# Attention pairs handled in groups of two, and weight sums formed in place, in a fused attention and feed-forward kernel

## The chip, the cores and the metric

The kernel runs on one core of one Trainium2 chip. The metric is the device time of one execution in microseconds. The kernel before took 860.98 us in the median of three runs (858.56 to 863.52).

## The reference

Sparse attention over 8 batches, 8 heads, 576 positions and head size 64, then a feed-forward layer on the result. Half of the heads look at the last 32 positions ("local"), half at earlier positions that are equal modulo 32 ("strided"):

```python
scores = scale * np.matmul(q, k.transpose(0, 1, 3, 2))
mask_local = (rel >= 0) & (rel < 32)
mask_strided = (rel >= 0) & (pos[None, :] % 32 == pos[:, None] % 32)
attn = softmax(np.where(masks, scores, -1e9))          # max subtracted, 1e-9 added to the sum
x = (attn @ v).transpose(0, 2, 1, 3).reshape(4608, 512)
h = x @ w_in                                           # 512 -> 2048
out = (h * sigmoid(1.702 * h)) @ w_out                 # 2048 -> 512
```

All arrays are float32.

## The kernel before, in words

The feed-forward matmuls use a Strassen-Winograd scheme with seven products in place of eight. Each float32 operand is split into a high and a low fp32r part, and a product is three matmuls per half of the contraction (high x high, high x low, low x high), six in all. The core's TensorE (PE) does one such group of six matmuls, 288 columns wide, per *step* `s` of a long list. Everything else is hung onto the steps: `side(s, f, ...)` puts `f` behind the product of step `s`, and every engine keeps the order in which the calls are made (`InOrder`). So the numbers given to `side` set the order on VectorE (DVE), ScalarE (ACT), GpSimd (POOL) and on SyncE's DMA queue (SP).

The stages:

- Start: the attention of batch 0, with filler matmuls.
- Steps 0 to `HEAD` - 1 = 60, and three more after it: batch 0 times `w_in` without Strassen (`plain`, 64 units of six matmuls each sum in two pieces), while the `w_in` words are turned into fp32 and split: `w_scale`, `w_low`, `w_join`, `w_high`, `w_low_part`. Each weight `i` is also stored to DRAM (`plains`) and read back later (`t_load`) into an area of the tile `sums`, where POOL forms four differences (`t_sums`), which ACT and DVE split into the weights `wv[i][:, 3:7]` (`t_high`, `t_low`).
- From step `HEAD`, seven passes of 56 steps, one for each batch 1 to 7: `product(n, k)`, k = 0 to 6, for n = 8 b + i. Product n starts at step 5 + 7 n and has a product at every second step, so two n are interleaved and each step has one product. The banks are `mx`, `my`, `mz` of set n % 2; `combine` empties them (ACT for k = 0 and 2, DVE for the others) and stores to `hid` in DRAM. A product that accumulates onto a bank has to wait until `combine` has read it: k = 5 in `my`, four steps after k = 3, is one.
- During the pass of batch b the attention of batch b + 1 is worked in six *pairs* (two 96-query chunks, or two sets of residues, of four heads), three local ("l") and three strided ("s"). The steps of a pair: `scores` (PE, into the PSUM banks `s0`, `s1`), `masked` and `maxima` (DVE), `below` (POOL subtracts the maximum), `exps` (ACT), `totals` (DVE), `scaled` (POOL), `turn` (PE transposes into `s0`, ACT copies out to `pts`), `values` (PE into `s0`, `s1`, ACT copies out into the blocks of the next x). `scores` and `values` are many small matmuls on parts of the PE array: 64 rows x 32 columns for local scores, 64 x 64 (or 54 x 64) for the rest.
- At the end of a pass the seven sums x of the next batch are made: `x_sum` (1, 2 on DVE; 3, 4 on POOL), `x_high` (ACT), `x_low` (DVE).
- Last: 72 groups of 42 matmuls with `w_out`, 256 columns wide; here a scheduler sets the order.

Of the kernel before, what the change touches and what calls it, by code (L numbers as in the profile page):

```python
# [9 lines left out]
F32 = mybir.dt.float32  # L10
# [46 lines left out]
def _pairs():  # L57
    out = []
    for b in range(B):
        x = [[(kind, b, U * i) for i in range(PAIRS // 2)] for kind in "ls"]  # L60
        out += x[0] + x[1] if b == 0 else [u for i in range(PAIRS // 2) for u in (x[1][i], x[0][i])]
    return out
# [8 lines left out]
def attn_ffn(ctx, tc, qk, vs, weights, masks, ident, out):  # L71
# [102 lines left out]
    def pr_of(p):  # L174
        return prs[(1, 2, 3, 0, 4, 5)[p] if p < PAIRS else p % 2]
# [39 lines left out]
    def scores(p, banks):  # L215
# [27 lines left out]
    def parts_of(p, banks):  # L243
# [6 lines left out]
            bank[:nq, : 4 * WL].rearrange("p (i n) -> p i n", i=4)[:, :, :nk] for bank in banks  # L250
# [14 lines left out]
    def masked(p, banks):  # L265
        nq, nk, mask, pr, heads, srcs, (nmax, _, _) = parts_of(p, banks)
# [54 lines left out]
    def values(p, banks, shared=False):  # L321

# [5 lines left out]
        for g in range(2):  # L328
            for w, (q0, n, _, nk) in enumerate(windows(kind)):
                if kind == "s":  # L330
                    n = min(n0, (w + 1) * WS) - w * WS
                for u in range(U):
                    i = U * g + u
                    o = g * n0 + (q0 if kind == "l" else w * WS)
                    for j in range(2):
# [6 lines left out]
                        )  # L342
        x = {k: xr[k].rearrange("p (g n) -> p g n", g=2) for k in ("11", "12", "21", "22")}
        for u in range(U):
            src = banks[u][:, : 2 * n0].rearrange("p (g n) -> p g n", g=2)
            copy = vector.tensor_copy if shared and u else scalar.copy
            if kind == "l":
                h, o = divmod(c + u, 3)
                copy(out=x[("11", "21")[h]][:, :, o * QL : (o + 1) * QL], in_=src)
                continue  # L350
            n, r0, half = RES[c], R0[c + u], NPOS // 2
            src = src.rearrange("p g (r t) -> p g t r", r=n)
            for k, h in enumerate(("12", "22")):
                o = x[h].rearrange("p g (t r) -> p g t r", r=STRIDE)[:, :, :, r0 : r0 + n]
                copy(out=o, in_=src[:, :, k * half : (k + 1) * half])
# [32 lines left out]
    KINDS = (0, 4, 1, 5, 3, 6, 2)  # L388
# [43 lines left out]
    def t_sums(i):  # L432
        b11, b21, b22, b12 = (t_view(0)[:, q] for q in range(4))
        t1, t2, t3, t4 = (t_view(1 + i % 2)[:, q] for q in range(4))
        for o, x, y in ((t1, b12, b11), (t2, b22, t1), (t3, b22, b12), (t4, b21, t2)):
            gpsimd.tensor_tensor(out=o, in0=x, in1=y, op=ALU.subtract)

    def t_high(i):
        scalar.copy(out=wv[i][:, 3:7, 0], in_=t_view(1 + i % 2))

    def t_low(i):
        hi, lo = (wv[i][:, 3:7, s] for s in range(2))
        vector.tensor_tensor(out=lo, in0=t_view(1 + i % 2), in1=hi.bitcast(F32), op=ALU.subtract)
# [3 lines left out]
    six = [m_banks[i][x] for x in ("mx", "my", "mz") for i in range(2)]  # L447
# [3 lines left out]
    def plain(n, u):  # L451
# [3 lines left out]
        bank = six[1 + 2 * f if j >= 4 * FP - 2 else j % 6][:, :HALF]  # L455
# [93 lines left out]
    for i in range(n0 + 3):  # L549
# [7 lines left out]
        if i >= 3:  # L557
            values(i - 3, s_banks, i == n0 + 2)
# [43 lines left out]

    for b in range(B):
        at = first(b)
        if b == 1:
            for t, f, k in ((-8, x_sum, 1), (-7, x_sum, 3), (-6, x_high, 4), (-5, x_low, 4),
                            (-5, x_sum, 2), (-4, x_high, 1), (-3, x_low, 1), (-3, x_high, 0),
                            (-2, x_low, 0), (-1, x_high, 2), (0, x_low, 2), (1, x_sum, 4),
                            (2, x_high, 3), (3, x_low, 3), (4, x_high, 6), (5, x_low, 6),
                            (6, x_high, 5), (7, x_low, 5)):  # L610
                side(at + t, f, k, b)
        elif b:
            side(at - 11, x_sum, 1, b)
            side(at - 10, x_sum, 3, b)
# [6 lines left out]
        for i in range(PAIRS if b + 1 < B else 0):  # L621
            p = (b + 1) * PAIRS + i
            s = at + 4 + 6 * i if b > 1 else at - 3 * b + 7 * i + 2 * (not b)
            t = (4, 5, 6, 9, 11) if b > 1 else (4, 5, 6, 11, 12) if b and not i else (5, 6, 7, 10, 12)
            side(s, scores, p, s_banks)
            side(s, load_qk, p + 2)
            for f, d in ((masked, 0), (maxima, 1), (below, 2), (exps, t[0]), (totals, t[1]), (scaled, t[2])):
                side(s + d, f, p, s_banks)
            side(s + t[3], turn, p, s_banks[0])
            side(s + t[4], values, p, s_banks)  # L630
            side(s + t[4], load_v, p + 2)
# [4 lines left out]
    for i in range(2, FP):  # L636
        at = 7 * (i - 2) + 4
        if i > 2:
            side(max(0, 7 * (i - 3) - 3), load_w, i)
# [324 lines left out]
```

## Time and profile before

| | before |
|---|---|
| time of the profiled execution | 858.98 us |
| its span, first to last instruction | 857.0 us |
| median of the runs | 860.98 us (858.56 to 863.52) |
| mean granted clock of TensorE | 0.993 |
| PE busy | 838.0 us (98% of the span) |
| PE weight loads busy | 808.8 us (94%) |
| DVE, POOL, ACT busy | 549.7, 490.9, 426.9 us |

The span starts with the first instruction and ends with the last; the 1.98 us between it and the execution's time lie around it. Busy times of one engine don't overlap with themselves, those of different engines do. In lists of instructions in order of time the columns are the start and the length in microseconds, engine, line, operation, what is written and read, the shape, and how many instructions the row merges; in brackets stands the idle time before them and what ended it. All recorded operations have the line of the helper `ordered`, so the tiles' names tell them apart: `mx`, `my`, `mz`, `s` are PSUM banks, `xa` the split x, `w` the split weights, `arena` most of the working memory.

### The profile page before, as it was taken

The page shows a single profiled execution, that of the slowest core. Times are in us where ns is not written, and L with a number is a line of the kernel's source. Part 1 is how long each engine was busy: PE and PEld are TensorE (multiplying, and loading weights), DVE is VectorE, ACT ScalarE, POOL GpSimd, SP SyncE. Part 2 cuts the span into 40 slices and gives each one's busy share as a digit, 9 for nine tenths or more (in the row PEclk, how much of TensorE's full clock was granted, in tenths as well). Part 3 has the DMA queues.
Part 4 walks back from the last instruction along what each step waited for, and adds up shares of the span by engine and source line. Part 5 has one row for each costly group of instructions (what it writes and reads, how often), then busy time and mean ns, then how long its engine had stood idle before and what let it go on. Part 6 is the DMA issues. An engine that isn't in the chain of part 4 may idle for free. (4 is left out here: it accounts for less than half of the span.)

```text
span 857.0 us, 23992 instructions
## 1 busy us (share of the span) xinstructions
PE 838.0 (98%) x9827; PEld 808.8 (94%) x9827; DVE 549.7 (64%) x867; ACT 426.9 (50%) x666; POOL 490.9 (57%) x509
## 2 busy tenths in 40 slices
PE   7899999999999999999999999999999999999997
PEld 4799898999999999999999999999999999999997
DVE  5575776965857658558577775665565565566662
ACT  4675444433444434434446564655555655655540
POOL 2233866242332342423344358999998998777760
PEclk9999999999999999999999999999999999999999
DMA  8897576576685765766768853444433433443430
GB/s 330 289 395 282 174 234 222 164 254 210 205 265 175 242 212 189 253 215 203 223 233 259 266 195 109 152 159 127 146 123 124 146 126 124 141 131 123 136 106 31
DMA packets 112239, 164.84 MB, mean 192 GB/s; under 512 B 9729, under 2 KB 88321, under 8 KB 111105
## 3 DMA queue, kind: packets, MB, share of 16 engines
q1 hardware_dynamic: 112128, 163.31, 58.5%
q8 instruction: 77, 1.26, 0.6%
q14 instruction: 34, 0.27, 0.1%
HBM read 104.55 MB, written 58.72 MB: 191 GB/s over the span
## 5 line engine op out<-in xcount | busy, mean ns | idle before, releaser
L87 POOL TENSOR_TENSOR arena<-arena 128x256 f32<-128x256 f32 (+1 forms) x302 | 332.3, 1117 | 127.3 <-ACT arena L87 54.5
L87 DVE TENSOR_TENSOR xa<-arena,xa 128x576 fp32r<-128x576 f32 (+2 forms) x100 | 158.8, 1589 | 87.6 <-ACT xa L87 56.4
L87 PE MATMUL my<-xa,w 128*128 128x288 f32 x1140 | 180.3, 300 | 0.5 <-DVE arena L87 0.4
L87 ACT ACTIVATE arena<-arena 128x1024 f32<-128x1024 f32 (+2 forms) x120 | 105.4, 878 | 125.7 <-DMA arena<-hid 93.7
L87 PEld LDWEIGHTS my<-xa,w 128*128 128x128 f32 x1140 | 158.7, 189 | 3.3 <-DVE arena L87 1.0
L87 ACT CAST xa<-arena 128x576 fp32r<-128x576 f32 (+2 forms) x102 | 115.5, 1147 | 38.2 <-PE s L87 25.1
L87 PE MATMUL mx<-xa,w 128*128 128x288 f32 x804 | 132.0, 301 | 2.5 <-DVE w L87 1.0
L87 PE MATMUL mz<-xa,w 128*128 128x288 f32 x792 | 128.4, 300 | 0.0
L87 ACT COPY arena<-mx 128x288 f32<-128x288 f32 (+1 forms) x136 | 53.7, 395 | 143.0 <-PE mx L87 107.9
L87 PEld LDWEIGHTS mx<-xa,w 128*128 128x128 f32 x804 | 113.5, 190 | 4.9 <-DVE w L87 1.3
L87 DVE TENSOR_TENSOR arena<-my,arena 128x288 f32<-128x288 f32 (+1 forms) x204 | 90.0, 446 | 41.0 <-PE my L87 39.3
L87 PEld LDWEIGHTS mz<-xa,w 128*128 128x128 f32 x792 | 110.9, 188 | 1.5
L87 POOL TENSOR_TENSOR arena<-arena,rinv 96x512 f32<-96x512 f32 (+1 forms) x48 | 49.5, 1031 | 107.6 <-DVE rinv L87 64.3
L87 DVE TENSOR_TENSOR arena<-mz,arena 128x288 f32<-128x288 f32 (+1 forms) x166 | 71.7, 441 | 51.8 <-PE mz L87 50.0
L87 ACT COPY arena<-s 128x90 f32<-128x90 f32 (+4 forms) x184 | 51.3, 340 | 82.5 <-PE s L87 82.1
L87 DVE TENSOR_TENSOR ga<-arena,ga 128x1792 fp32r<-128x1792 f32 (+1 forms) x25 | 57.4, 2297 | 51.6 <-ACT ga L87 40.6
L87 POOL TENSOR_TENSOR arena<-arena,nmax 128x432 f32<-128x432 f32 (+1 forms) x42 | 46.3, 1103 | 76.7 <-DVE nmax L87 72.7
L87 PE MATMUL mz<-w_out,xa 128*128 128x256 f32 x576 | 75.5, 280 | 0.0
L87 PE MATMUL mx<-w_out,xa 128*128 128x256 f32 x576 | 75.4, 280 | 0.0
L87 PE MATMUL my<-w_out,xa 128*128 128x256 f32 x576 | 75.3, 280 | 0.0
L87 PEld LDWEIGHTS mx<-w_out,xa 128*128 128x128 f32 x576 | 71.1, 188 | 0.0
L87 PEld LDWEIGHTS my<-w_out,xa 128*128 128x128 f32 x576 | 71.0, 188 | 0.0
(72 smaller groups left out, 1000.8 us busy)
## 6 DMA issues: line engine op xcount, KB each, us to landing
hid<-arena SPq DMA_DIRECT2D x256, 144.0 KB, 3.2
arena<-hid SPq DMA_DIRECT2D x144, 256.0 KB, 3.3
arena<-qk SPq DMA_DIRECT2D x23, 448.0 KB, 4.5
arena<-qk SPq DMA_DIRECT2D x21, 472.0 KB, 4.4
arena<-vs SPq DMA_DIRECT2D x23, 384.0 KB, 4.6
out<-arena SPq DMA_DIRECT2D x34, 256.0 KB, 2.9
raw<-w_in SPq DMA_DIRECT2D x8, 1024.0 KB, 10.1
stage<-w_out SPq DMA_DIRECT2D x16, 512.0 KB, 5.1
```

The lines of the kernel that those rows point to most:

```text
L87: ins = call(*args, **kw)
```

## The change

1. **Pairs in groups of two.** The local and the strided pair of a group are scored in one step, side by side in the banks `s0`, `s1` (columns 0 and 256). The values of both pairs stand in one step, ahead of the scores of the next group, and go to two product banks, `mx1` and `mz0`, instead of `s0`, `s1`. So a step that held one of `scores` or `values` of one pair now holds up to four of them. Each pair's `turn` has a step of its own, as before, three and one (two for batch 1) steps ahead of the values. `moved` holds the copies out of the values. The local pair comes first.
2. **`plain` uses four banks in place of six** (the other two hold values), and DVE copies out for weights 0 to 4, ACT for 5 to 7 (before: one half each).
3. **Weight sums in place.** Each `plains[i]` is read into one of three areas, and the four differences overwrite it. The steps of load, four sums, high and low part come from a table, counted from `HEAD` (`T_STEPS`; one `t_sum(i, m)` is one difference), and the order of the weights is another (`KINDS`). For n = 8, product 1 goes ahead of product 0.
4. **Weights are prepared every 6 steps** in place of 7, and `w_low_part` of weights 1 to 7 runs on POOL in two halves. For batch 1, `x_low` of 4 and 6 runs on POOL, and the steps of its sums are earlier.

```diff
-        return prs[(1, 2, 3, 0, 4, 5)[p] if p < PAIRS else p % 2]
+        return prs[(1, 2, 3, 0, 4, 5)[p] if p < PAIRS else 1 - p % 2]
...
-    def scores(p, banks):
+    def scores(p, banks, at=0):
-                        banks[j][q0 : q0 + n, i * WL : i * WL + nk],
+                        banks[j][q0 : q0 + n, at + i * WL : at + i * WL + nk],
...
-                            banks[u][j * D : (j + 1) * D, o : o + n],
+                            banks[u][j * D : (j + 1) * D, at + o : at + o + n],
+        return lambda u: moved(p, u, banks[u][:, at : at + 2 * n0], shared)
...
-    def w_low_part(i):
-        hi, lo = (wv[i][:, 0:4, s] for s in range(2))
-        vector.tensor_tensor(out=lo, in0=words[i], in1=hi.bitcast(F32), op=ALU.subtract)
+    def w_low_part(i, some=slice(0, 4)):
+        hi, lo = (wv[i][:, some, s] for s in range(2))
+        (gpsimd if i else vector).tensor_tensor(
+            out=lo, in0=words[i][:, some], in1=hi.bitcast(F32), op=ALU.subtract
+        )
...
-        sync.dma_start(out=t_view(0), in_=plains[i].rearrange("p (q n) -> p q n", q=4))
+        sync.dma_start(out=t_view(i % 3), in_=plains[i].rearrange("p (q n) -> p q n", q=4))
-        for o, x, y in ((t1, b12, b11), (t2, b22, t1), (t3, b22, b12), (t4, b21, t2)):
+        o, x, y = ((b11, b12, b11), (b12, b22, b12), (b22, b22, b11), (b21, b21, b22))[m]
+        gpsimd.tensor_tensor(out=o, in0=x, in1=y, op=ALU.subtract)
...
-    six = [m_banks[i][x] for x in ("mx", "my", "mz") for i in range(2)]
+    four = [m_banks[0]["mx"], m_banks[0]["my"], m_banks[1]["my"], m_banks[1]["mz"]]
+    v_banks = [m_banks[1]["mx"], m_banks[0]["mz"]]
-            (vector.tensor_copy if f else scalar.copy)(out=h, in_=bank)
+            (vector.tensor_copy if n < 5 else scalar.copy)(out=h, in_=bank)
...
+    def both_scores(q):
+        for i in range(2):
+            scores(q + i, s_banks, 256 * i)
+            load_qk(q + i + 2)
+    def both_values(p):
+        moves = []
+        for i in range(2):
+            moves.append(values(p + i, v_banks, False, 216 * i))
+            load_v(p + i + 2)
+        for u in range(U):
+            for move in moves:
+                move(u)
+    def groups_of(b, slots):
+        for g in range(3):
+            q, s, then = b * PAIRS + 2 * g, slots[g], slots[g + 1]
+            side(s, both_scores, q)
+            for i in range(2):
+                side(s + i, masked, q + i, s_banks, 256 * i)
+                for f, d in (
+                    (maxima, 0), (below, 0), (exps, 4), (totals, 5 + i), (scaled, 5 + i)
+                ):
+                    side(s + d + i, f, q + i, s_banks)
+                side(then - (3, 2 if b == 1 else 1)[i], turn, q + i, s_banks[i])
+            side(then, both_values, q)
...
+            groups_of(b + 1, [at + t for t in ((3, 16, 30, 44) if b else (3, 17, 32, 47))])
...
-        at = 7 * (i - 2) + 4
+        at = 6 * (i - 2) + 4
+        for t in (0, 2):
+            side(at + 6 + t, w_low_part, i, slice(t, t + 2))
+    T_STEPS = (
+        (-19, (-15, -14, -13, -12), -10, -5), (-18, (-10, -9, -8, -7), -4, 1),
```

Three places in the order of the instructions show what moved.

PE, in a pass, around the values of a first group (`s0`, `s1`: scores, and before also values; `ident`: `turn`; rows with `xa` and `w`: a product of six matmuls). Before:

```order
L87 MATMUL s0_82<-arena_66 64x32 x2
...
L87 MATMUL mz0_78<-xa_67,w_2_636 128x288 x6
L87 MATMUL s0_82<-arena_66 32x64
...
L87 MATMUL my1_80<-xa_67,w_3_757 128x288 x6
L87 MATMUL my0_77<-xa_67,w_2_636 128x288 x6
L87 MATMUL mx1_79<-xa_67,w_3_757 128x288 x6
L87 MATMUL s0_82<-ident_sb_72,arena_66 128x128 x4
L87 MATMUL mz0_78<-xa_67,w_2_636 128x288 x6
L87 MATMUL my1_80<-xa_67,w_3_757 128x288 x6
L87 MATMUL s0_82<-arena_66 64x54 x2
...
L87 MATMUL mx0_76<-xa_67,w_4_874 128x288 x6
L87 MATMUL s0_82<-arena_66 64x54
```

Now:

```order
L87 MATMUL s0_82<-ident_sb_72,arena_66 128x96 x4
L87 MATMUL mx0_76<-xa_67,w_2_670 128x288 x6
L87 MATMUL mz1_81<-xa_67,w_1_550 128x288 x6
L87 MATMUL s1_83<-ident_sb_72,arena_66 128x128 x4
L87 MATMUL my0_77<-xa_67,w_2_670 128x288 x6
L87 MATMUL mx1_79<-arena_66 64x32 x2
...
L87 MATMUL mx1_79<-arena_66 64x54 x2
...
L87 MATMUL s0_82<-arena_66 32x64
...
L87 MATMUL s0_82<-arena_66 64x54
...
L87 MATMUL my1_80<-xa_67,w_1_550 128x288 x6
```

Four runs of small matmuls, each between products, became one: local values (64x32), strided values (64x54 and the like), local scores (32x64), strided scores (64x54). A batch has 4 such runs (scores; values and scores; the same; values) where it had 12; the six `turn` stay apart.

DVE, at the first steps of a pass (`xa`: `x_low`; `s0`, `s1` and `nmax`: `masked` and `maxima`; `my`, `mz`: `combine`). Before:

```order
L87 TENSOR_TENSOR arena_66<-my1_80,arena_66 128x288
L87 TENSOR_TENSOR xa_67<-arena_66,xa_67 128x576
L87 SCALAR_TENSOR_TENSOR arena_66<-s0_82,masks_sb_71 128x4x54
L87 SCALAR_TENSOR_TENSOR arena_66<-s1_83,masks_sb_71 128x4x54
L87 TENSOR_TENSOR arena_66<-mz1_81,arena_66 128x288
L87 TENSOR_TENSOR xa_67<-arena_66,xa_67 128x576
L87 TENSOR_REDUCE nmax_30_3989<-arena_66 128x8
L87 TENSOR_TENSOR arena_66<-my0_77,arena_66 128x288
L87 TENSOR_TENSOR xa_67<-arena_66,xa_67 128x576
```

Now:

```order
L87 TENSOR_TENSOR arena_66<-my1_80,arena_66 128x288
L87 TENSOR_TENSOR xa_67<-arena_66,xa_67 128x576
L87 SCALAR_TENSOR_TENSOR arena_66<-s0_82,masks_sb_71 96x4x64
L87 SCALAR_TENSOR_TENSOR arena_66<-s1_83,masks_sb_71 96x4x64
L87 TENSOR_REDUCE nmax_30_4011<-arena_66 96x8
L87 SCALAR_TENSOR_TENSOR arena_66<-s0_82,masks_sb_71 128x4x54
L87 SCALAR_TENSOR_TENSOR arena_66<-s1_83,masks_sb_71 128x4x54
L87 TENSOR_REDUCE nmax_31_4027<-arena_66 128x8
L87 TENSOR_TENSOR arena_66<-mz1_81,arena_66 128x288
L87 TENSOR_TENSOR xa_67<-arena_66,xa_67 128x576
L87 TENSOR_TENSOR arena_66<-my0_77,arena_66 128x288
```

Two pairs are masked in a row, ahead of the same `combine` of `mz1` and `my0`; `x_low` and `combine` keep their steps.

POOL, around step `HEAD` (`sums`: `t_sum`; 128x576: `x_sum` 3 and 4, with `xa` `x_low`; `nmax`: `below`; `rinv`: `scaled`; `w_7`: `w_low_part`). Before:

```order
L87 TENSOR_TENSOR arena_66<-arena_66,rinv_11_1147 96x4x128
L87 TENSOR_TENSOR sums_1273<-sums_1273 128x256 x4
L87 TENSOR_TENSOR arena_66<-arena_66 128x576
L87 TENSOR_TENSOR sums_1273<-sums_1273 128x256 x4
L87 TENSOR_TENSOR arena_66<-arena_66,nmax_12_1403 128x4x2x54
L87 TENSOR_TENSOR arena_66<-arena_66 128x576
```

Now:

```order
L87 TENSOR_TENSOR w_7_1170<-raw_7_901,w_7_1170 128x2x256 x2
L87 TENSOR_TENSOR sums_1206<-sums_1206 128x256 x4
L87 TENSOR_TENSOR arena_66<-arena_66 128x576
L87 TENSOR_TENSOR sums_1206<-sums_1206 128x256 x4
L87 TENSOR_TENSOR xa_67<-arena_66,xa_67 128x576
L87 TENSOR_TENSOR sums_1206<-sums_1206 128x256 x5
L87 TENSOR_TENSOR arena_66<-arena_66 128x576
L87 TENSOR_TENSOR sums_1206<-sums_1206 128x256
L87 TENSOR_TENSOR arena_66<-arena_66,nmax_12_1497 96x4x128
```

Between the two `x_sum` of batch 1 (rows 128x576) stood four sums; now nine, and an `x_low`.

More of the change, by code (lines that the diff above doesn't have):

```diff
@@ L60, in _pairs @@
         x = [[(kind, b, U * i) for i in range(PAIRS // 2)] for kind in "ls"]
[L61 removed]
+        out += x[0] + x[1] if b == 0 else [u for i in range(PAIRS // 2) for u in (x[0][i], x[1][i])]
     return out
@@ L249, in parts_of @@
         srcs = [
-            bank[:nq, : 4 * WL].rearrange("p (i n) -> p i n", i=4)[:, :, :nk] for bank in banks
+            bank[:nq, at : at + 4 * WL].rearrange("p (i n) -> p i n", i=4)[:, :, :nk]
+            for bank in banks
         ]
@@ L263, in each, with masked @@
         return t.unsqueeze(3).broadcast_to([t.shape[0], 4, 2, nk])
-    def masked(p, banks):
-        nq, nk, mask, pr, heads, srcs, (nmax, _, _) = parts_of(p, banks)
+    def masked(p, banks, at=0):
+        nq, nk, mask, pr, heads, srcs, (nmax, _, _) = parts_of(p, banks, at)
         if p < PAIRS:
@@ L342, in values, with moved @@
                         )
+        return lambda u: moved(p, u, banks[u][:, at : at + 2 * n0], shared)
+    def moved(p, u, src, shared):
+        kind, _, c = pairs[p]
         x = {k: xr[k].rearrange("p (g n) -> p g n", g=2) for k in ("11", "12", "21", "22")}
[L344 to L355, printed above, removed]
+        src = src.rearrange("p (g n) -> p g n", g=2)
+        copy = vector.tensor_copy if shared and u else scalar.copy
+        if kind == "l":
+            h, o = divmod(c + u, 3)
+            copy(out=x[("11", "21")[h]][:, :, o * QL : (o + 1) * QL], in_=src)
+            return
+        n, r0, half = RES[c], R0[c + u], NPOS // 2
+        src = src.rearrange("p g (r t) -> p g t r", r=n)
+        for k, h in enumerate(("12", "22")):
+            o = x[h].rearrange("p g (t r) -> p g t r", r=STRIDE)[:, :, :, r0 : r0 + n]
+            copy(out=o, in_=src[:, :, k * half : (k + 1) * half])
     halves = {k: t.rearrange("p (c n) -> p c n", c=2) for k, t in xr.items()}
@@ L454, in plain @@
         j = 4 * n + 2 * r + f
-        bank = six[1 + 2 * f if j >= 4 * FP - 2 else j % 6][:, :HALF]
+        bank = (v_banks[0] if j == 4 * FP - 4 else four[j % 4])[:, :HALF]
         w = wv[n].rearrange("p k s (c m) -> p k s c m", c=2)
@@ L620, in attn_ffn @@
             side(at, x_sum, 4, b)
[L621 to L631, printed above, removed]
+        if b + 1 < B:
+            groups_of(b + 1, [at + t for t in ((3, 16, 30, 44) if b else (3, 17, 32, 47))])
     def word(f, i):
@@ L636, in attn_ffn @@
     for i in range(2, FP):
-        at = 7 * (i - 2) + 4
+        at = 6 * (i - 2) + 4
         if i > 2:
-            side(max(0, 7 * (i - 3) - 3), load_w, i)
+            side(max(0, 6 * (i - 3) - 3), load_w, i)
         side(at, word, w_scale, i)
         side(at + 1, word, w_low, i)
-        for t, f in ((3, w_join), (4, w_high), (6, w_low_part)):
+        for t, f in ((3, w_join), (4, w_high)):
             side(at + t, f, i)
-    for i in range(FP):
-        at = HEAD - 10 + STEP * i
-        for t, f in ((-3, t_load), (0, t_sums), (6, t_high), (8, t_low)):
-            side(at + t, f, i)
+        for t in (0, 2):
+            side(at + 6 + t, w_low_part, i, slice(t, t + 2))
+    T_STEPS = (
[4 rows of a table added]
+    )
+    for i, (load, sums, high, low) in enumerate(T_STEPS):
+        for m in range(4):
+            side(HEAD + sums[m], t_sum, i, m)
+        for t, f in ((load, t_load), (high, t_high), (low, t_low)):
+            side(HEAD + t, f, i)
     last = first(B - 1)
@@ L841, in attn_ffn @@
                 if not odd and 0 <= k < 7 and n >= FP:
-                    product(n, k)
-                    combine(n, k)
+                    early_one = n == FP and k < 2
+                    product(n, 1 - k if early_one else k)
+                    if early_one and k == 0:
+                        continue
+                    for m in range(2) if early_one else (k,):
+                        combine(n, m)
         for f, a in sides.pop(s, ()):
```

34 lines of the change are left out of this document (17 added, 17 removed), and 3 rows, old and new, of the table T_STEPS.

## The prediction

> **What bounds the kernel now.** The page first: PE is busy all the time, and no other engine is near it.
>
> ```profile
> span 857.0 us, 23992 instructions
> PE 838.0 (98%) x9827; PEld 808.8 (94%) x9827; DVE 549.7 (64%) x867; ACT 426.9 (50%) x666; POOL 490.9 (57%) x509
> ```
>
> A busy share says nothing of whether PE does useful work, so next the stages, cut where the list in order of time shows the first scores of a batch (columns: stretch, its length, PE, weight loads, DVE, ACT, POOL, clock, DMA share, GB/s):
>
> ```profile
> 31.70:81.00 49.30, 49.01 (x742) 46.30 (x734) 35.82 (x59) 35.13 (x63) 16.23 (x12) 1.00 0.90 328
> ...
> 160.03:217.42 57.39, 57.39 (x841) 54.73 (x841) 39.34 (x83) 23.88 (x59) 20.18 (x26) 1.00 0.70 219
> 217.42:274.82 57.40, 57.40 (x841) 54.73 (x841) 39.29 (x83) 23.86 (x59) 20.19 (x26) 1.00 0.69 219
> ...
> 491.10:857.00 365.90, 359.58 (x3026) 358.97 (x3024) 213.87 (x205) 196.26 (x160) 295.12 (x272) 0.99 0.41 129
> ```
>
> From 160 on a pass takes 57.4 us again and again, with PE busy throughout at the full clock; DVE has 39.3 us of it, ACT 23.9, POOL 20.2. There only fewer or denser PE instructions can shorten anything. The waits of PE between 31.7 and 491 are few (total, times, longest; one more of 0.4 lies in the last pass, which the change leaves alone):
>
> ```profile
> PE s L87 <- POOL arena L87: 1.5, 3, 1.0
> PE mx L87 <- DVE xa L87: 0.7, 1, 0.7
> PE mx L87 <- ACT xa L87: 0.7, 1, 0.7
> ```
>
> So what the passes lose on PE is not idle time. It shows in the order of time, where a run of small matmuls (`s`) stands between two products:
>
> ```profile
> 286.29 1.05 PE L87 MATMUL my<-xa,w 128*128 128x288 f32 x6
> 287.27 0.69 PE L87 MATMUL s<-arena 64*64 64x54 f32 x32
> 287.89 1.06 PE L87 MATMUL my<-xa,w 128*128 128x288 f32 x6
> 288.79 0.96 PE L87 MATMUL mx<-xa,w 128*128 128x288 f32 x6
> 289.59 0.95 PE L87 MATMUL mz<-xa,w 128*128 128x288 f32 x6
> ```
>
> Read the distances of starts. An undisturbed product takes 289.59 - 288.79 = 0.80. The one after the run takes 0.90, and the one from 286.29, which stands after a run and before one, 0.98. So a product pays 0.10 after and 0.08 ahead of a run. The run itself pays too, as the only place shows where two runs stand side by side, in the start of the kernel:
>
> ```profile
> 12.24 0.69 PE L87 MATMUL my<-early 64*64 64x54 f32 x32 [0.68 <-DMA early<-qk]
> 12.75 0.86 PE L87 MATMUL s<-arena 64*64 64x32 f32 x48
> 13.54 0.39 PE L87 MATMUL mz<-arena 128*128 128x512 bf16 x1
> ...
> 292.43 0.90 PE L87 MATMUL s<-arena 64*64 64x32 f32 x48
> 293.26 1.06 PE L87 MATMUL mz<-xa,w 128*128 128x288 f32 x6
> ```
>
> The same 32 matmuls take 0.51 (12.24 to 12.75) when another run follows, 0.62 (287.27 to 287.89) when a product does: 0.11 for leaving. The 48 of local values take 0.79 after a run, 0.83 after a product: 0.04 for entering. A run between products costs 0.10 + 0.08 + 0.11 + 0.04 = 0.33 us beyond its own work.
>
> **The change part by part.** Fewer runs: 12 a batch become 4, over seven batches 84 become 28. 56 x 0.33 = 18.5 us go, all on PE, and nothing hides PE there. `turn` keeps its six places. The matmuls are the same in number and shape.
>
> Inside a joined run the kinds of tile change: values and strided scores use 64x64 tiles, local scores 64x32. In the order there are five such changes a batch (one, two, two, none), 35 in all. No row shows one. The row at 12.24 has neighbours of one tile kind and no price, which gives 0 as one end; a full 0.33 is the other. I take 0.15, the part that a run itself pays at its ends (0.11 + 0.04), since the 0.18 paid by products is that of whole-array matmuls. 35 x 0.15 = 5.2; ends 0 and 11.6. PE gains 18.5 - 5.2 = 13.3 (6.9 to 18.5).
>
> The Trainium skill, "TensorEngine Tiling (Array Packing)", Key Properties, says that changing the tiling mode, not just the tile, drains TensorE. By it the 35 changes are not free and the gain is the 13.3; by the row at 12.24 alone, where nothing drains, it would be 18.5. The trace has no such change to decide it.
>
> DVE at a pass's opening. Scores of the first group come at the fourth step, while `x_low` is still under way; now two pairs are masked in a row, ahead of the `combine` of k = 3, which frees `my` for k = 5. The rows of this place before:
>
> ```profile
> 272.93 1.76 DVE L87 TENSOR_TENSOR xa<-arena,xa 128x576 fp32r<-128x576 f32 x1
> 274.62 0.81 DVE L87 TENSOR_TENSOR arena<-my,arena 128x288 f32<-128x288 f32 x2
> 275.35 0.75 DVE L87 TENSOR_TENSOR xa<-arena,xa 128x576 fp32r<-128x576 f32 x1
> 276.01 0.66 DVE L87 SCALAR_TENSOR_TENSOR arena<-s,masks_sb 128x216 f32<-128x216 f32 x2
> 276.60 0.44 DVE L87 TENSOR_TENSOR arena<-mz,arena 128x288 f32<-128x288 f32 x1
> 276.96 0.74 DVE L87 TENSOR_TENSOR xa<-arena,xa 128x576 fp32r<-128x576 f32 x1
> 277.63 0.59 DVE L87 TENSOR_REDUCE nmax<-arena 128x8 f32<-128x432 f32 x1
> 278.14 0.44 DVE L87 TENSOR_TENSOR arena<-my,arena 128x288 f32<-128x288 f32 x1
> ...
> 272.64 1.44 POOL L87 TENSOR_TENSOR arena<-arena 128x576 f32<-128x576 f32 x1 [6.97 <-DVE xa L87]
> ```
>
> DVE is already late here: it has no gap. The same operations now stand in the same order, with the local pair's mask and maximum ahead of them. By the distances of starts those of the strided pair take 0.59 + 0.51 = 1.10 (276.01 to 276.60, 277.63 to 278.14); local has 256 columns in place of 216, so 1.3. And `below` of both pairs runs on POOL beside the `x_low` that follows; the row at 272.93 shows what that does: 1.76 in place of 0.75 while POOL works from 272.64 to 274.08, so x_low may wait for most of a `below`, 0.7. The `combine` that ended at 278.58 then ends at 278.58 + 1.3 + 0.7 = 280.6. PE wants k = 5 six products after the scores: they begin one product earlier than 274.82, at 274.0, and take about 1.3 (0.62 strided, about as much local, 0.15 for the change of tile, less the 0.11), then 0.1 and six products of 0.80: 280.2. A wait of 0.4 in the five passes 2 to 6: 2.0 us (0 if `x_low` gets ahead of POOL, 0.8 each and 4 if both `below` block it).
>
> Around step `HEAD`. The waits that are there before, and rows of POOL, ACT and DVE for a pair and for the weight sums:
>
> ```profile
> 95.09 0.40 PE L87 MATMUL mx<-xa,w 128*128 128x288 f32 x1 [0.74 <-ACT xa L87]
> 96.24 0.93 PE L87 MATMUL mx<-xa,w 128*128 128x288 f32 x5 [0.75 <-DVE xa L87]
> 144.19 0.55 PE L87 MATMUL s<-ident_sb,arena 96*128 96x96 f32 x4 [1.05 <-POOL arena L87]
> ...
> 94.03 4.41 POOL L87 TENSOR_TENSOR sums<-sums 128x256 f32<-128x256 f32 x4 [2.81 <-DMA sums<-plains]
> 124.24 1.04 POOL L87 TENSOR_TENSOR arena<-arena,nmax 96x512 f32<-96x512 f32 x1
> 125.31 0.63 ACT L87 ACTIVATE arena<-arena 96x512 f32<-96x512 f32 x1 [1.14 <-POOL arena L87]
> 125.97 0.69 DVE L87 TENSOR_REDUCE ssum<-arena 96x8 f32<-96x520 f32 x1 [1.00 <-ACT arena L87]
> 127.04 1.04 POOL L87 TENSOR_TENSOR arena<-arena,rinv 96x512 f32<-96x512 f32 x1 [1.76 <-DVE rinv L87]
> 128.24 1.21 DVE L87 TENSOR_TENSOR w<-sums,w 128x1024 fp32r<-128x1024 f32 x1
> 129.51 2.94 POOL L87 TENSOR_TENSOR sums<-sums 128x256 f32<-128x256 f32 x4 [1.43 <-DMA sums<-plains]
> 242.82 0.65 ACT L87 COPY arena<-s 128x90 f32<-128x90 f32 x4 [0.53 <-PE s L87]
> 249.80 0.54 ACT L87 COPY arena<-s 128x192 f32<-128x192 f32 x2 [0.75 <-PE s L87]
> ```
>
> With the other POOL waits of PE at `turn` they make 1.5 + 0.74 + 0.75 = 3.0 us. The x sums now stand four steps (3.2 us) earlier, and product 1 goes ahead of 0, so the first two waits go; the sums, loaded three steps ahead before, now mostly have five and more, so POOL waits less for DMA and the third goes. New: POOL is crowded there. `x_sum` 3 can begin when step 47 (0.8), its values (0.83 + 0.62), their copies (0.65 + 0.54) and `x_sum` 1 (0.75) are over, 4.2 us after step 46. From there to the `x_low` of product 6 POOL has 12 sums of 0.74 (2.94 / 4), four of 128x576 (1.44) and two `below` (1.04): 8.8 + 5.8 + 2.1 = 16.7. DVE works against it with four `x_low` (0.75) and two `t_low` (1.21), 5.4; in the row at 94.03 four sums took 1.5 longer beside some 3 us of such work, so half of it counts: 2.7. POOL is done at 4.2 + 16.7 + 2.7 = 23.6; PE wants it after 26 products (20.8), the values, the scores and their ends, at about 23.7. With no margin I take 1.0 of waits, and 0.2 where product 1 meets a late copy out of `my` by ACT: 1.2 (0 to 4). Net 3.0 - 1.2 = 1.8 gained (3.0 gained to 1.0 lost).
>
> At no cost: `w_low_part` on POOL (16.2 of 49.3 us busy in that stage; two of about 1.3, as 512 is to 576, a weight; if late, they delay weight i, which has 2 i steps in hand); the same work taken from DVE, which bounds nothing; the shift of `hid` copies between ACT and DVE, with four banks in place of six (DVE has 13.5 us free in that stage; a bank is written again after five more steps, 4.0 us, and two pairs' masks block DVE for 2.4); six value copies in a row on ACT (1.2; the two banks rest from the 12th to the 21st step of the pass, values come at the 16th); two loads of q and k together on SP (used 13 steps or 10 us later); `t_load` of weight 3, which waits on SP for `t_low` of weight 0, with `hid` stores behind it whose buffers come round after ten steps or so; the other numbering of the weights, and of `prs`. The last 366 us begin with the last products and move with them.
>
> Sum: 858.98 - 13.3 + 2.0 - 1.8 = 845.9 for an execution like the profiled one, which lies 2.0 under the median of the runs; from the median it is 847.9. I say 847.
>
> **The rivals.**
> Tile changes inside a run are free: then 858.98 - 18.5 + 2.0 - 1.8 = 840.7. For it, the row at 12.24; against it, that the weights of the other tile kind cannot be loaded ahead while the first still runs, as at the ends of a run.
> Tile changes cost as much as a whole run's ends, and POOL is late around `HEAD`: 858.98 - 6.9 + 4 + 1.0 = 856. For it, the margin of 0.1 in the POOL sum; against it, that the products' 0.18 of the 0.33 has no product to fall on.
> The values wait (slower): a step of values now needs both `pts`, so a late `scaled` of the second pair holds PE at its `turn`, one product ahead. Place: the 21 groups; price: the 1.05 at 144.19, so 21 x 1.05 = 22 and 858.98 - 13.1 + 22 = 868. It decides from (13.1 + 4.3) / 21 = 0.83 each. For it, the crowding of POOL and DVE above. Against it, twelve steps or 9.6 us from scores to `turn`, and in them masks and maxima of both pairs 2.4, `below` 1.0, `exps` 0.6, `totals` 0.9 with the reciprocal, `scaled` 1.0: 5.9.
> That the runs aren't joined is excluded by the order of the instructions.
>
> **How the numbers follow.** 0.5% (4.3 us) is about what a measurement can tell from no change. Chances: the sum as it stands, 842 to 852: 0.60; free changes, 839 to 842: 0.15; dear changes with waits, 852 to 856: 0.12; waits that take nearly all, 857 to 865: 0.06; the values wait, slower: 0.07. Faster 0.87, same 0.06, slower 0.07. The range 840 to 855 leaves out the last two, a third of the free case and a part of the dear one, 2 in 10.
>
> **What would show it.** A pass of batch 2 to 6 should be 57.4 - 8 x 0.33 + 5 x 0.15 + 0.4 = 55.9 long; four runs in it, the middle ones 2.6 to 2.9 us from product to product; at a change from 64x64 to 64x32 a distance between 0 and 0.33, which settles the first two rivals; a wait of PE for DVE at k = 5 six products after the first scores; none at `turn` from batch 2 on; the waits at the first two products of batch 1 gone. The prediction fails if PE waits at values or `turn` in each group, or if the passes get longer than 57 us.

## The result, and the profile after

The changed kernel takes 867.43 us in the median (863.10 to 871.11), the kernel before 860.78 (858.56 to 863.52): a ratio of 1.0079, with a 95% interval of 1.0059 to 1.0098. It is slower by 0.8%; 847 was forecast. The profiled execution took 864.59 us, 5.6 more than the one of before. Its page opens so:

```profile
span 862.8 us, 23915 instructions
PE 828.2 (96%) x9821; PEld 807.0 (94%) x9827; DVE 539.6 (63%) x862; ACT 424.3 (49%) x662; POOL 507.3 (59%) x524
```

PE has 9.8 us less of busy time and 5.8 us more of span: the work did get cheaper, and PE now waits. The waits of PE between 31.7 and 500 us (total, times, longest; `issue` is idle time in which PE waited for nothing that the profile shows), where before there were four kinds with 3.3 us in all:

```profile
PE s L87 <- issue: 6.5, 6, 1.6
PE my L87 <- DVE arena L87: 4.3, 7, 0.8
PE my L87 <- DVE xa L87: 2.2, 1, 2.2
PE my L87 <- ACT arena L87: 2.1, 1, 2.1
PE mx L87 <- ACT arena L87: 2.1, 2, 1.5
PE my L87 <- POOL w L87: 1.2, 2, 0.7
PE s L87 <- POOL arena L87: 0.6, 1, 0.6
PE mx L87 <- POOL w L87: 0.2, 1, 0.2
```

The stages next, each cut at the same products in both kernels (columns as in the windows above). The first fence is of the kernel before, from the first product with `w_in` into the pass of batch 1:

```profile
28.42:152.00 123.58, 119.52 (x1717) 112.03 (x1716) 84.73 (x145) 67.20 (x137) 62.95 (x60) 0.99 0.76 265
```

The changed kernel: the same stretch, two of the five passes in question, the stage of `w_out`:

```profile
28.55:158.57 130.02, 118.11 (x1716) 112.89 (x1716) 80.49 (x140) 65.41 (x132) 84.94 (x75) 0.97 0.74 254
222.23:281.18 58.95, 56.20 (x841) 54.44 (x841) 38.20 (x83) 23.80 (x59) 20.34 (x27) 1.00 0.64 214
337.61:394.01 56.40, 55.67 (x842) 54.21 (x841) 38.87 (x83) 23.79 (x59) 20.04 (x27) 1.00 0.68 224
498.85:862.80 363.95, 358.10 (x3026) 357.49 (x3024) 211.50 (x205) 196.04 (x160) 287.55 (x272) 1.00 0.41 130
```

The stage around `HEAD` lost 6.4 us. Of the five passes, three take 56.4 (1.0 less than the 57.4 of before) and two nearly 59; together they lost 0.4. The last pass lost 0.8; the `w_out` stage is 1.95 shorter, mostly for a reason given below (the clock) that is not the change. 0.1 + 6.4 + 0.4 + 0.8 - 1.95 = 5.8.

What makes two passes long is seen in the order of time, in a run of values and scores. Undisturbed, and disturbed:

```profile
295.86 0.23 PE L87 MATMUL mz<-arena 54*64 54x54 f32 x2
295.91 0.23 PE L87 MATMUL mx<-arena 54*64 54x54 f32 x2
295.92 0.23 PE L87 MATMUL mz<-arena 54*64 54x54 f32 x2
296.07 1.35 PE L87 MATMUL s<-arena 64*32 64x64 f32 x80
297.36 1.06 PE L87 MATMUL my<-xa,w 128*128 128x288 f32 x6
...
237.13 0.71 PE L87 MATMUL s<-arena 64*32 64x64 f32 x46
239.41 0.91 PE L87 MATMUL s<-arena 64*32 64x64 f32 x34 [1.57 <-issue]
240.26 1.07 PE L87 MATMUL my<-xa,w 128*128 128x288 f32 x6
```

The same 80 matmuls take 1.29 us (296.07 to 297.36) or 3.13. In the second run PE stands still for 1.57 us in the middle, and no engine is named. Was the instruction itself not there yet? Counted in the program's order, the six stalls come at matmul 1743, 1998, 3399, 3654, 5947 and 6202: distances of 255, 1401, 255, 2293 and 255, all multiples of 127.4. With as many weight loads that is 255 instructions, nearly 256. The trace has 9821 matmuls and 9827 loads of PE, 77 times 255; with 73 further records of PE's sequencer it is 77 times 256. The page has 77 packets, of 16 KB each, on a queue of instructions (packets, MB, share):

```profile
q8 instruction: 77, 1.26, 0.6%
```

So PE's instructions seem to come in blocks of 256, one packet each. For the stall above, the block before it ends at 235.59 (matmul 3272); a packet begins 1.4 us later and lasts from 236.99 to 237.92; PE's idle time lasts from 237.84 to 239.41, so PE goes on 1.5 us after the packet. It is alike in all six: a packet begins 0.3 to 1.5 us after the end of the block before and takes 0.9 to 1.0, and PE goes on 1.2 to 1.5 us after the packet's end. The block's own work is 2.2 to 2.3 us each time, so by and large the stall is the longer, the later the packet begins: 0.45 us at 0.34 after the block's end, 1.57 at 1.40.

### The profile page after: what moved, and what is told of

The parts are those of the page before. It is cut to its first block, busy times and chain, and to the rows that moved or that the text cites. A ratio compares the mean times of both kernels' runs of the same rounds, so it can differ in the third digit from the quotient of the medians.

```text
span 862.8 us, 23915 instructions
## 1 busy us (share of the span) xinstructions
PE 828.2 (96%) x9821; PEld 807.0 (94%) x9827; DVE 539.6 (63%) x862; ACT 424.3 (49%) x662; POOL 507.3 (59%) x524
## 5 line engine op out<-in xcount | busy, mean ns | idle before, releaser
L87 POOL TENSOR_TENSOR arena<-arena 128x256 f32<-128x256 f32 (+1 forms) x302 | 326.9, 1099 | 143.8 <-ACT arena L87 62.5
L87 PE MATMUL my<-xa,w 128*128 128x288 f32 x1200 | 191.0, 299 | 10.0 <-DVE arena L87 4.3
L87 PEld LDWEIGHTS my<-xa,w 128*128 128x128 f32 x1200 | 167.6, 189 | 13.9 <-ACT arena L87 7.0
L87 ACT COPY arena<-mx 128x288 f32<-128x288 f32 (+4 forms) x196 | 65.4, 358 | 187.1 <-PE mx L87 142.4
L87 PE MATMUL mx<-xa,w 128*128 128x288 f32 x768 | 127.3, 301 | 1.2 <-DVE w L87 1.0
L87 PE MATMUL mz<-xa,w 128*128 128x288 f32 x768 | 124.1, 297 | 0.0
L87 PEld LDWEIGHTS mx<-xa,w 128*128 128x128 f32 x768 | 109.9, 191 | 2.2 <-DVE w L87 1.3
L87 POOL TENSOR_TENSOR arena<-arena,nmax 96x512 f32<-96x512 f32 (+1 forms) x42 | 42.1, 1004 | 95.1 <-DVE nmax L87 90.9
L87 PEld LDWEIGHTS mz<-w_out,xa 128*128 128x128 f32 x576 | 70.9, 188 | 0.0
```

The source lines that it names most:

```text
L87: ins = call(*args, **kw)
```

## The experiments

**Is it the supply of instructions?** Theory A: when a block ends, the one after the next is fetched, and PE stops if it is through before that has come. The blocks that ended in the six stalls were worked off in 2.2 us; from 160 us to the end of the passes no other took less than 4.3. Two edits test it. The first puts two products between values and scores:

```diff
-            q, s, then = b * PAIRS + 2 * g, slots[g], slots[g + 1]
+            q, s, then = b * PAIRS + 2 * g, slots[g] + (2 if g else 0), slots[g + 1]
```

> The changed kernel, but the scores of a group stand two steps behind the values of the group before (two products lie between them; everything of the group that counts from its scores moves by the same two steps). A run of values is then 48 matmuls and a run of scores 80, in place of 128 in a row. Theory A: the stalls of PE put down to 'issue' (six between 31.7 and 490 us, 6.5 us in all) come from PE's instructions not being fetched in time, because 128 small matmuls and their 128 weight loads use up one fetched block of 256 instructions in 3 us, faster than the next one comes (about 3.5 us from the crossing of a block's end). Then the six stalls go. The 14 more runs cost 14 x (0.33 - 0.15) = 2.5 us, since a tile change goes for each. Against the changed kernel that is -6.5 + 2.5 = -4.0 us: 1.003 to 1.004 of the kernel before. Rival: the stalls come at the ends of blocks whatever runs there, or from a crowded DMA: they stay at 5 to 7 us, and the kernel is slower by the 2.5 us: 1.011 of the kernel before.

Measured: 862.68 us, 1.0031 (1.0017 to 1.0045), as theory A has it, and no `issue` among its waits of PE. Each pass now takes the same:

```profile
273.70:330.50 56.80, 56.07 (x843) 54.28 (x841) 40.16 (x82) 23.80 (x60) 20.00 (x26) 1.00 0.68 215
```

56.8 against 56.4 is the forecast price of two more runs and two tile changes less (0.36). The second edit leaves the runs long and moves the instructions:

```diff
         late = all_banks[4 + i % 2]
+        if i == 0:
+            for _ in range(64):
+                matmul(late[:, :16], lhsT=zeros[:, :P], rhs=zeros[:, :16], start=True, stop=True)
```

> The changed kernel with 64 tiny matmuls (16 columns, of zeros) more at the very start, where PE waits for the first inputs; the rest is the same. They move every later instruction of PE by 128 places, half a block of 256. Theory A (PE stops where a block of 256 instructions ends less than some 3.5 us after the one before): the stalls move. In the changed kernel they fell at matmul 1743, 1998, 3399, 3654, 5947 and 6202, all a multiple of 127.4 matmuls apart, each in a block that was used up in 2.2 us; blocks of 3.7 us and more had none. With the ends of blocks 64 matmuls earlier in the program the blocks that are used up in 2.2 us are those that end in the values and scores of the first batch's pass at about 181 and 196 us: stalls of 1 to 1.6 us there, at most 0.5 us at about 296, 311, 355 and 370, and none at 124, 140, 239, 255, 412 and 427. Rival (the stall belongs to these places, by their data or the DMA traffic there): the same six places as before.

Measured (one run, 862.77 us): all six stalls are gone from their places. Two stand elsewhere, one in a run and one at the second product behind a run:

```profile
199.15 0.55 PE L87 MATMUL s<-arena 64*64 64x54 f32 x19 [0.68 <-issue]
355.77 1.06 PE L87 MATMUL mx<-xa,w 128*128 128x288 f32 x6 [0.56 <-issue]
```

They are at matmul 2889 and 5182, ends of blocks by the same count, near 196 and 355 us as forecast. The first is smaller than the 1 to 1.6 forecast, the second a little over the 0.5, and the one forecast at 181 didn't come: the block from 181.5 to 183.5 was worked off in 2.0 us without a stall, and the last packet before had begun at 180.43, 1.1 us ahead of it. So the cause is shown: a joined run of 128 matmuls and 128 weight loads is as long as a block, and where an end of a block falls near the run's start, PE can outrun the fetch. Whether it does, and for how long, goes with the time at which the packet begins; what sets that time, no run here shows.

**Which part costs the 6.4 us around `HEAD`?** The groups only, from the changed kernel:

```diff
-    KINDS = (0, 5, 1, 6, 3, 4, 2)
+    KINDS = (0, 4, 1, 5, 3, 6, 2)
-        at = 6 * (i - 2) + 4
+        at = 7 * (i - 2) + 4
...
```

Not shown in it: `w_low_part`, `t_load` to `t_low` and their steps, the x sums of batch 1, the copies of `plain` and the order of products at n = 8 are as before too.

> The changed kernel with the groups of two, but with the weights prepared as before: every 7 steps, low parts on DVE, sums into areas of their own at the old steps, the old order of the weights, the copies of the plain products split between DVE and ACT, the x sums of batch 1 at their old steps. Theory B: the waits of PE between 31.7 and 160 us that were not there before (for POOL at w 1.4, for ACT at values 2.1, for ACT at product 1 2.1, for DVE xa 2.2) come from the new pace and table of the weights, not from the groups. Then they fall from 8.5 to about 3 us, and the time by 5 to 6 us against the changed kernel: 1.001 to 1.002 of the kernel before, with the issue stalls still there. Rival: the groups crowd DVE, ACT and POOL there by themselves: waits of 8 us or more stay, 1.006 to 1.012.

Measured: 868.13 us, 1.0092 (1.0060 to 1.0124). The weights only, on the kernel before (the same lines the other way):

> The kernel before, with its single pairs, and only the weight part of the change: every 6 steps, low parts on POOL in two halves, sums in place in three areas with the table of steps, the new order of weights and of the sums of batch 1, DVE's and ACT's copies as in the change. Theory B (the weight part makes the new waits before 160 us): slower than before by 5 to 6 us, 1.006 to 1.007, with PE waits for POOL w, ACT arena and DVE xa between 31.7 and 160 us as in the changed kernel, and no issue stall. Rival (the groups make them): 0.996 to 1.001, since the 3.0 us of waits of before at this place go or stay.

Measured: 863.07 us, 1.0028 (1.0014 to 1.0042), between the two forecasts. Theory B falls: the groups alone cost as much as the whole change (1.0092 and 1.0079, and their intervals overlap). The stage, cut at the same products, with groups only:

```profile
29.08:161.93 132.85, 119.58 (x1718) 113.66 (x1717) 89.29 (x145) 67.47 (x137) 59.23 (x60) 0.96 0.71 246
```

With the weights only:

```profile
28.98:155.24 126.26, 120.10 (x1717) 113.43 (x1715) 81.17 (x140) 65.00 (x129) 83.76 (x74) 0.97 0.75 259
```

Before 123.6, groups alone 132.9, weights alone 126.3, both 130.0. The weight part costs 2.7 by itself and takes 2.9 off what the groups cost (9.3). A part of these differences is the clock: in these stages the traces have one stretch of 3.41 us at half clock before, three with the groups alone, two with the weights alone and two in the changed kernel, each worth up to 1.7 us (below). With groups alone the largest wait is of PE for the first x, and POOL shows why:

```profile
99.82 0.61 PE L87 MATMUL mx<-xa,w 128*128 128x288 f32 x1 [4.19 <-ACT xa L87]
...
91.77 3.33 POOL L87 TENSOR_TENSOR sums<-sums 128x256 f32<-128x256 f32 x4 [10.27 <-DMA sums<-plains]
```

POOL waited for the weights read back from `plains`, whose load stands on SP behind the loads of two pairs at once, and the `x_sum` behind it on POOL was late. The table of the change moves that load to 19 steps ahead of `HEAD`, after which this wait isn't there, and brings waits of its own, which rest on ACT and POOL in the changed kernel:

```profile
65.79 1.05 ACT L87 CAST w<-raw 128x1024 fp32r<-128x1024 f32 x1 [3.99 <-POOL w L87]
66.74 1.12 ACT L87 ACTIVATE raw<-raw 128x1024 f32<-128x1024 f32 x1
67.76 0.47 ACT L87 COPY arena<-s 128x384 f32<-128x384 f32 x1
...
68.28 0.25 PE L87 MATMUL mx<-arena 64*64 64x32 f32 x2 [1.46 <-ACT arena L87]
98.59 1.33 PE L87 MATMUL my<-xa,w 128*128 128x288 f32 x6 [2.10 <-ACT arena L87]
112.13 1.01 PE L87 MATMUL my<-xa,w 128*128 128x288 f32 x5 [2.20 <-DVE xa L87]
...
109.19 2.88 DVE L87 TENSOR_TENSOR xa<-arena,xa 128x576 fp32r<-128x576 f32 x1 [1.06 <-ACT xa L87]
109.37 0.73 POOL L87 TENSOR_TENSOR sums<-sums 128x256 f32<-128x256 f32 x1
110.06 1.40 POOL L87 TENSOR_TENSOR xa<-arena,xa 128x576 fp32r<-128x576 f32 x1
```

At 65.79 `w_high` stands on ACT for 4 us, until POOL is done with the low part of an earlier weight (in the code raw words and split weights share one pool of rooms); behind it waits the copy of `turn` at 67.76, and for that the values at 68.28. At 98.59 product 1 waits for ACT's copy out of `my`, which stands behind `t_high` and `x_high`. At 112.13 a product waits for an `x_low` that took 2.88 us in place of 0.75, beside three operations of POOL; it ended 0.61 us after the last of them. Low parts back on DVE, on the kernel with scores two steps behind:

```diff
-        (gpsimd if i else vector).tensor_tensor(
+        vector.tensor_tensor(
-        for t in (0, 2):
-            side(at + 6 + t, w_low_part, i, slice(t, t + 2))
+        side(at + 6, w_low_part, i)
```

> The kernel with scores two steps behind the values, and the low parts of the w_in weights made on DVE in one piece, as in the kernel before, in place of POOL in two. Theory C: the waits of PE between 35 and 90 us (5.3 us there: for POOL at w, for POOL at turn, for ACT at values) come from the low parts on POOL. They keep the raw tile whose room the next weight's high part needs, so ACT stands still behind that (4.0 us at 65.8 us in the changed kernel) with the copies of turn behind it, and POOL's below and scaled come late. Then 4 to 5 us go: 0.997 to 0.999 of the kernel before. Rival: DVE, with 8 us more work there, is late in its place: 1.002 to 1.005.

Measured: 860.56 us, 1.0014 (0.9999 to 1.0030), against 1.0031 (1.0017 to 1.0045) of the kernel it edits: 1.5 us by the ratios, less than half of the forecast, and their intervals overlap. The stage fell from 129.4 (first line) to 126.5:

```profile
30.69:160.07 129.38, 119.36 (x1717) 111.46 (x1716) 80.64 (x140) 65.32 (x129) 83.21 (x74) 0.98 0.73 248
30.61:157.07 126.46, 117.04 (x1715) 109.81 (x1715) 86.21 (x147) 65.78 (x129) 67.13 (x61) 1.00 0.75 254
```

Its waits of PE ahead of 161 us: those for `w` (0.8) went; of 5.3 us for POOL at `turn` 4.1 stayed, and one of 1.3 for DVE came. All waits of that stage together fell only from about 10 to 9.2 us. Most of the rest is the clock: the first trace has a stretch of half clock at 86.19, behind two such waits, and the second has none in this stage. So the low parts on POOL explain some 0.8 us of waits, and at most the 2.9 if that stretch was their doing: theory C in small part.

**The wait at k = 5.** In the changed kernel it is where the prediction put it, in each of five passes:

```profile
286.55 0.95 PE L87 MATMUL my<-xa,w 128*128 128x288 f32 x6
288.22 1.03 PE L87 MATMUL my<-xa,w 128*128 128x288 f32 x6 [0.73 <-DVE arena L87]
```

First attempt, both masks of a pass's first group later:

```diff
+            o = 3 if g == 0 and b > 1 else 0
+            e = 2 if o else 0
-                side(s + i, masked, q + i, s_banks, 256 * i)
+                side(s + o + i, masked, q + i, s_banks, 256 * i)
-                    (maxima, 0), (below, 0), (exps, 4), (totals, 5 + i), (scaled, 5 + i)
+                    (maxima, o), (below, o), (exps, 4 + e), (totals, 5 + e + i), (scaled, 5 + e + i)
```

> The kernel with scores two steps behind the values, and in the passes the masks and maxima of the first group 3 steps later, so that they stand behind the combine of k = 3 on DVE (exps, totals and scaled of that group 2 steps later; its scores and its turns stay). Theory D: the wait of PE for DVE at k = 5, 0.73 us in each of five passes, comes from the masks of two pairs ahead of that combine. Then it goes, and part of the 2.4 us of waits at 112 to 117 us too, where below and x_low slow each other: -3.7 to -5 us, 0.997 to 0.999 of the kernel before. Rival: the x_low beside POOL's work make DVE late, or the first group's turn now waits, some 0.7 us a pass: 1.001 to 1.004.

Measured: 869.12 us, 1.0102 (1.0080 to 1.0124), above both forecasts. The wait went and two came, in each of the five passes:

```profile
293.69 1.07 PE L87 MATMUL mz<-xa,w 128*128 128x288 f32 x6 [0.58 <-DVE arena L87]
296.43 0.55 PE L87 MATMUL s<-ident_sb,arena 96*128 96x96 f32 x4 [0.88 <-POOL arena L87]
```

Theory D names the right cause and the edit moves it: now the `combine` of `mz` stands behind the masks, and `turn` is reached before `scaled`. With low parts on DVE and the copies of weight 7 too:

```diff
-            (vector.tensor_copy if n < 5 else scalar.copy)(out=h, in_=bank)
+            (vector.tensor_copy if n < 5 or n == 7 else scalar.copy)(out=h, in_=bank)
```

> Both of the two edits above, and the last plain products (weight 7) copied out by DVE instead of ACT, where a copy stood behind t_high on ACT, which waited for POOL (2.1 us at product 1 of the changed kernel). If theories A, C and D hold and their costs add up: 862.7 - 4.5 - 4.5 - 0.5 = 853, 0.991 to 0.993 of the kernel before. If the waits only move from one engine to the next: 0.998 to 1.003.

Measured: 867.22 us, 1.0089 (1.0070 to 1.0109), above both forecasts: waits moved on, not away (PE waits 9.5 us for POOL at `turn`).

**Groups only where they fit.** The kernel before up to the pass of batch 1, groups for batches 3 to 7, and of a first group only the strided pair masked later:

```diff
+GROUPS = 3
+GAP = 2
...
-        for i in range(PAIRS if b + 1 < B else 0):
+        if GROUPS <= b + 1 < B:
+            groups_of(b + 1, [at + t for t in (3, 16, 30, 44)])
+        for i in range(PAIRS if b + 1 < min(B, GROUPS) else 0):
...
+                o, e = (2, 1) if g == 0 and i else (0, 0)
```

> The kernel before up to the pass of batch 1 (single pairs for the attention of batches 0 to 2, its way and pace of the weights), and groups of two only for the attention of batches 3 to 7, in the five passes of batches 2 to 6; scores stand two steps behind the values of the group before. In the first group of a pass only the local pair is masked at its old step; the strided pair's mask, maximum and below come 2 steps later, behind the combine of k = 3 (its exps, totals and scaled 1 later). Theory E: all of what the changed kernel lost before 160 us comes from groups and weights crowded around step HEAD, and none of it is needed for the gain in the passes. Then the stages up to 160 us are as long as before, the pass of batch 2 to 6 gains 0.6 as in the split kernel and the 0.73 of the wait at k = 5: 5 x 1.33 = 6.7 us, 0.992 of the kernel before. Rivals: the wait at k = 5 stays or moves to another bank, as with both masks late (0.58 + 0.88 a pass): 0.996 to 1.001; or the later part needs the weights' new order to be fast, and waits come there: over 1.001.

Measured: 852.16 us (851.12 to 854.16), 0.9918 (0.9900 to 0.9935), faster than both kernels. The stage around `HEAD` is no longer than the 123.58 of before:

```profile
30.89:153.57 122.68, 118.69 (x1717) 111.18 (x1715) 83.27 (x145) 66.60 (x133) 62.92 (x59) 0.99 0.75 262
```

With `GAP = 0`, and then with the 64 matmuls more:

> The same, with the scores in the step of the values again: runs of 128 small matmuls. Theory A: each pass is 0.4 us shorter for two runs less, and the stalls 'issue' come back where a block of 256 PE instructions is used up in 2.2 us. The count of PE's instructions ahead of the passes is that of the changed kernel, so they fall at nearly the same matmuls as there, 3399, 3654, 5947 and 6202, with 0.4 to 1.6 us each and 4 us in all: -5 x 1.73 + 4 = -4.6 us, 0.994 to 0.996 of the kernel before. Rival (the stalls belong to the crowded stage before): none, -8.6 us, 0.990.

> The same as the one with scores in the step of the values, and 64 tiny matmuls of zeros more at the very start, while PE waits for inputs. Theory A: the ends of blocks then fall 64 matmuls earlier in the program; in the five passes with groups this put one stall of 0.6 us (at 356 us) in place of four with 4.1 us. Then -8.6 + 0.6 = -8 us, 0.990 to 0.992 of the kernel before, and below the kernel with scores two steps behind. Rival: as without the 64, 0.994 to 0.996.

Measured: 852.11 us, 0.9912 (0.9895 to 0.9928), and 855.87 us, 0.9956 (0.9940 to 0.9972). An undisturbed pass with `GAP = 2`:

```profile
209.51:265.44 55.93, 55.93 (x842) 54.28 (x841) 39.52 (x82) 23.82 (x60) 21.18 (x26) 1.00 0.71 225
```

And with `GAP = 0`:

```profile
210.23:265.75 55.52, 55.52 (x842) 54.20 (x841) 38.20 (x82) 23.77 (x60) 21.11 (x26) 1.00 0.68 227
```

PE has no wait in them (two steps apart, one stall of 0.31 us is left in all five passes): theory E holds. The stalls came back in the joined form, 1.9 us in three places in place of the forecast 4 us in four, and only two were forecast ones (matmul 5943 and 6198; the third is 4287), so that joining gained nothing measurable over two steps apart. Moving the instructions made it worse here, against the forecast: stalls at 2886, 5179 and 5434, the last two of 1.8 and 1.3 us, and behind the first of these two a stretch of half clock. The ends of blocks lay some 10 matmuls away from those of the changed kernel with 64 more (5182 there, in a trace that lacks 7 matmuls of the start), where the last two places had cost 0.56 and nothing. The packets differ with the stalls: at 5943 and 6198 a packet had begun 0.5 and 0.1 us before the end of the block before (stalls of 0.36 and 0.30), at 5179 it began 1.6 us after it (1.83). A joined run depends on a few instructions anywhere ahead of it, and on when the next block is fetched.

**The clock.** The kernel before again, for the clock of each run:

> The kernel before, unchanged, for the granted clock of each of its runs. Ten runs of the changed kernel had clocks of 0.980 to 0.998, and the times went with them (863.1 us at 0.998, 871.1 at 0.980). If the clock is the chip's own affair, the kernel before shows the same spread of clocks and of times, some 8 us; if the changed kernel, with its denser stretches of small matmuls, draws a lower clock, the kernel before stays at 0.992 or more and within 5 us. Ratio 1.000 either way.

Measured: 859.63 us, 0.9987 (0.9973 to 1.0001), clocks of 0.988 to 0.998 and times of 857.5 to 861.5, against 0.980 to 0.998 and 863.1 to 871.1 for the changed kernel: half the spread in time, but clocks below the 0.992 of the second forecast, so neither forecast fits whole. In the traces the clock is 1.0 but for stretches at 0.50 of 3.41 us or, in the first 110 us, two to five times that in a row (17.07 from 15.70 in this run, while the kernel starts), and a piece at the very end. The changed kernel around 98.59:

```profile
98.59:102.60 4.01, 4.01 (x18) 4.01 (x19) 3.53 (x3) 0.52 (x1) 3.85 (x4) 0.57 0.64 192
```

Its products there, in order of time:

```profile
99.72 1.64 PE L87 MATMUL mz<-xa,w 128*128 128x288 f32 x6
101.16 1.60 PE L87 MATMUL mx<-xa,w 128*128 128x288 f32 x6
```

After the wait of 2.10 a product takes 1.44 in place of 0.80. The half clock begins at 99.18 for 3.41 us and costs half of that, 1.7; a second follows the wait at 112.13. Before has one here, at 97.56, behind its two waits of 0.7, and one at 524.23 in the `w_out` stage behind a wait of 1.73; there the changed kernel waits 1.72 and has none, which accounts for 1.7 of the 1.95 by which that stage is shorter. One stretch is 0.002 of the mean clock of a run, so by an estimate from these the changed kernel has one to ten in a run, before one to six, those at the start included: whether a wait of this length brings one differs from run to run. That more waits bring more of them fits; it was not tried apart from the waits.

## Why the prediction was wrong

- **A round trip at 0.33 and a tile change at 0.15: right.** A clean pass with all runs joined takes 55.52, 1.88 less than before; 8 x 0.33 - 5 x 0.15 = 1.89. In the changed kernel it is 57.40 - 56.40 + 0.73 = 1.73. Both rivals on the tile changes fall: free changes would give 2.64, dear ones 0.99. The row of 296.07 shows one change by itself: the first local score starts 0.15 after the last value (295.92), where inside the values 0.05 lie between such rows (295.86 to 295.91), so it costs about 0.1. That the sum agrees to 0.01 is therefore partly luck; each price alone is good to some hundredths. (The dear rival's sum in the prediction is added wrongly: 858.98 - 6.9 + 4 + 1.0 is 857.1, not 856; nothing else rests on it.)
- **DVE at a pass's opening: right place and engine, size wrong.** 0.73 a pass in place of 0.4, so 3.7 for 2.0.
- **Around `HEAD`: this step failed.** It had waits of 3.0 before and 1.2 after; measured are 8.4 and 2.3 of stalls, and a second stretch of half clock, 1.7. With the share of two batches in the runs' gain I had this stage 5.6 shorter; it is 6.4 longer: 12 of the 18.7 us that I missed. The POOL sum was not the part that decided. Low parts on POOL stood under "at no cost", with two steps in hand for each weight: but they hold the room that ACT's next `w_high` needs, and what stands behind it on ACT (values waited 2.1 us for ACT in the changed kernel, 1.0 with scores two steps behind, 0.6 with the low parts on DVE too). Copies out of `my` on ACT got 0.2 and took 2.1. `x_low` beside POOL counted only for what it adds to POOL's time; it took 2.88 for 0.75 itself, and a product waited 2.2 for it. The loads of two pairs together, at no cost too, held `plains` back with groups alone.
- **The supply of instructions: missing.** I asked of a joined run only what its ends cost. The stalls are 6.5 us in the trace, and a pass with two of them is 2.5 longer; two such passes are 5.0 of the 7.9 us by which the five passes missed the forecast.
- **"The values wait"**, the slower rival, named the right kind of wait, but it came in one group (1.46 and 0.63), not in 21. The change is slower for other reasons.
- What is not settled: the groups' own 9.3 us around `HEAD` are read from one trace (the loads of two pairs ahead of `plains` on SP), not tried by an edit. Nor were the single waits of the changed kernel there, but for the low parts. What is shown is that the gain of the passes needs neither: with groups and the new weight part left out of it the stage is as long as before (122.68).

## What to carry to other kernels

A gain per run, found in clean rows, held here in the stages that look like those rows, and not where three engines were crowded; carry it out there alone first, and leave the crowded stage as it is. For each operation moved "at no cost", ask whose room it holds until it is done, and what is queued behind the one that waits for that room. When very small instructions are put together, count them against the block in which an engine's instructions arrive.

## What the runs showed of the hardware that I had not expected

- PE's instructions come in blocks (255 counted, 16 KB a packet). In each of the 21 stalls in the traces of six kernels here PE went on 1.2 to 1.6 us after the end of such a packet; the six blocks worked off in 2.2 us in the changed kernel cost a stall of 0.45 to 1.57 each, and one of 2.0 us cost none where its packet had come early (at 181.5, with 64 matmuls more). The Trainium skill, "Runtime: NRT & Kernel Launch", Instruction fetch mechanics, has the block of 256 instructions, fetched while the one before is worked. The trace agrees with the size; the page's remark that the fetch is hidden does not hold for runs of small matmuls here.
- In the changed kernel two waits of about 2 us (2.10 and 2.20) were each followed by 3.41 us at half clock, and so cost nearly twice their length; one of 1.72 was not. The Trainium skill, "TensorE: Matmul & The Clock Gate", Part 1, gives such a window and a half clock after an idle one; here 2.1 us without work were enough.
- A subtraction on DVE (128x576) took 2.88 us beside POOL's operations and 0.75 alone. In 35 of the 36 rows in which it began beside an operation of POOL, in the traces of both kernels, it ended 0.60 to 0.62 us after the end of one: by these rows it waited for POOL, at 109.19 through three operations in a row.
